# First pair's queries in a causal-attention and token-mixing kernel: one transfer and a turn on TensorE in place of four blocks and a turn on VectorE

## The chip, the cores and the metric

The kernel runs on one core of a Trainium2 chip. A core has five engines with their own in-order instruction streams (TensorE or PE for matrix products, VectorE or DVE, ScalarE or ACT, GpSimd or POOL, SyncE or SP, which here only issues transfers), and 16 DMA engines that carry the transfers of all queues. The metric is the time of one execution on the device in microseconds; lower is better.

## The reference

Inputs are q, k and v of shape (4, 12, 448, 64) and four weight matrices, all float32 (the token weights arrive as 8-byte floats and are narrowed in the kernel). Causal attention is followed by a mixer over tokens and one over channels:

```python
scores = q @ k.transpose(0, 1, 3, 2) / sqrt(64)          # 448 x 448 for each of 48 heads
scores = where(triu(ones, 1), -1e9, scores)
attn = exp(scores - max) / (sum + 1e-9)
x = (attn @ v).transpose(0, 2, 1, 3).reshape(4, 448, 768)
xt = x.transpose(0, 2, 1)
h = maximum(xt @ w_tok1, 0) @ w_tok2                      # over tokens: 448 -> 256 -> 448
u = x + h.transpose(0, 2, 1)
out = u + maximum(u @ w_ch1, 0) @ w_ch2                   # over channels: 768 -> 1536 -> 768
```

## The kernel before, in words

Heads are taken in 24 pairs: the 64 values of one head lie on partitions 0 to 63, of the other on 64 to 127. For each pair `load_pair` loads keys, queries and values; `prep` turns keys and queries so that the head dimension lies on partitions; `heads` makes the scores (line 1021, 32 small products in two jobs), masks them on VectorE (line 1043), takes exponentials on ScalarE (line 1055), sums and norms; `by_tensor` (pairs 0 to 9, line 1115) or `by_dma` turns the probabilities; `values` multiplies them with the values (lines 1245 and 1254). `xturn` and `tokens` mix tokens each time two head pairs of a batch are done (a third of its channels), and `channels` and `group` do the channel products (lines 1433, 1765, 1836, 1860), the bulk of the span. Everything is accumulated in PSUM and copied or added out of it by VectorE or ScalarE.

Keys and queries are turned in one of two ways. In the one of pair 0 and of pairs 6 and up, `load_pair.blocks` loads each tensor of a pair in four transfers (line 940) so that 32x32 blocks lie in place, and VectorE turns the blocks (`prep.turn`, line 988). In that of pairs 1 to 5 (`0 < g < WHOLE`), `load_rows` loads rows as they lie, in one transfer for pairs 1 and 2 (line 892, `g < ONCE`) and two for pairs 3 to 5 (line 895); TensorE turns them by products with the identity (`turn_rows.turn`, line 916 for pairs 1 and 2, 910 from pair 3), and VectorE or ScalarE copies the result out of PSUM (`turn_rows.evac`, through the helper `copy`, lines 632 and 634). Values are loaded by `load_pair.load` in three transfers (lines 949 and 953), and `load_pair.upper` copies a small part of them. `narrow` loads token weights (line 686).

The order of work is planned when the kernel is built. Each step is a job with costs, needs and buffers. `Plan.emit` walks a planned clock: each time an engine is free, it takes the ready job of lowest rank. The rank of a job is its place in a written list, `PLACES`, keyed by step, by the step's own number (twice the pair's number plus a constant) and by count; where several engines can do a job, a second list, `CHOICE`, gives the letter of the engine (a ScalarE, d VectorE, p GpSimd, s SyncE). Each engine runs its jobs in the order that the plan wrote. Constants of the plan are a transfer's lead (1320 ns), its time to land (1050 ns), and lags from engine to engine (145 ns from ScalarE).

Where the plan finds no ready job for TensorE in the first 75 us and little activity of late, it writes a filler (`keep_warm`, line 865): a product of 512 columns whose result is never read.

In pair 0, the keys go out on SyncE's queue and the queries on ScalarE's; the values of pair 0 follow on SyncE's queue, those of pair 1 on ScalarE's.

Of the kernel before, what the change touches and what calls it, by code (L numbers as in the profile page):

```python
# [21 lines left out]
    "load_pair.blocks": {-2: (0, 1), 10: (129, 153), 12: (193, 224), 14: (242, 259), 16: (338, 293), 18: (405, 420),  # L22
        20: (522, 537), 22: (578, 591), 24: (670, 694), 26: (742, 758), 28: (831, 851), 30: (911, 927), 32: (996,
        1006), 34: (1056, 1070), 36: (1141, 1151), 38: (1205, 1220), 40: (1280, 1293), 42: (1333, 1348), 44: (1406,
        1426)},
    "load_pair.load": {0.5: (2,), 2.5: (3,), 4.5: (178,), 6.5: (209,), 8.5: (274,), 10.5: (312,), 12.5: (393,),
        14.5: (453,), 16.5: (490,), 18.5: (558,), 20.5: (615,), 22.5: (704,), 24.5: (773,), 26.5: (822,), 28.5:
        (902,), 30.5: (949,), 32.5: (1047,), 34.5: (1114,), 36.5: (1194,), 38.5: (1241,), 40.5: (1376,), 42.5:
        (1441,), 44.5: (1489,), 46.5: (1531,)},
    "load_pair.upper": {-0.2: (12,), 1.8: (15,), 3.8: (213,), 5.8: (245,), 7.8: (317,), 9.8: (380,), 11.8: (441,),  # L30
        13.8: (505,), 15.8: (519,), 17.8: (592,), 19.8: (651,), 21.8: (727,), 23.8: (821,), 25.8: (859,), 27.8:
        (938,), 29.8: (982,), 31.8: (1077,), 33.8: (1136,), 35.8: (1226,), 37.8: (1269,), 39.8: (1401,), 41.8:
        (1462,), 43.8: (1517,), 45.8: (1561,)},
    "narrow.load": {3.5: (6, 9, 16, 62, 86, 121, 114, 144), 12: (288,), 13: (371,), 14: (445,), 15: (503,), 16:
        (606,), 17: (665,), 18: (755,), 19: (818,), 20: (897,), 21: (974,), 22: (1041,), 23: (1120,), 24: (1191,),
        25: (1254,), 26: (1328,), 27: (1400,), 28: (1463,), 29: (1511,), 30: (1553,), 31: (1599,), 32: (1627,), 33:
        (1660,), 34: (1687,), 35: (1730,)},
    "narrow.size": {3.5: (32, 52, 61, 116, 133, 177, 180, 235), 12: (352,), 13: (413,), 14: (484,), 15: (545,), 16:
        (642,), 17: (705,), 18: (786,), 19: (854,), 20: (932,), 21: (1013,), 22: (1072,), 23: (1153,), 24: (1223,),
        25: (1291,), 26: (1360,), 27: (1437,), 28: (1497,), 29: (1532,), 30: (1584,), 31: (1616,), 32: (1646,), 33:  # L40
        (1676,), 34: (1712,), 35: (1748,)},
    "narrow.shift": {3.5: (37, 56, 73, 125, 142, 183, 186, 263), 12: (359,), 13: (424,), 14: (491,), 15: (554,), 16:
        (646,), 17: (710,), 18: (793,), 19: (863,), 20: (939,), 21: (1019,), 22: (1084,), 23: (1157,), 24: (1227,),
        25: (1295,), 26: (1371,), 27: (1446,), 28: (1503,), 29: (1538,), 30: (1588,), 31: (1621,), 32: (1649,), 33:
        (1678,), 34: (1720,), 35: (1750,)},
    "narrow.join": {3.5: (40, 63, 80, 131, 146, 187, 194, 298), 12: (364,), 13: (436,), 14: (497,), 15: (587,), 16:
        (652,), 17: (724,), 18: (796,), 19: (870,), 20: (948,), 21: (1024,), 22: (1089,), 23: (1161,), 24: (1234,),
        25: (1300,), 26: (1374,), 27: (1450,), 28: (1505,), 29: (1543,), 30: (1590,), 31: (1623,), 32: (1655,), 33:
        (1681,), 34: (1725,), 35: (1755,)},
    "token_weights.<lambda>": {3.5: (44, 69, 85, 135, 150, 191, 201, 303)},  # L50
    "token_weights.rest_of": {3.5: (50, 74, 89, 139, 156, 195, 206, 310)},
    "prep.turn": {-1.5: (5, 8), 10.5: (199, 216), 12.5: (253, 271), 14.5: (286, 304), 16.5: (375, 384), 18.5: (449,
        486), 20.5: (562, 577), 22.5: (609, 626), 24.5: (702, 734), 26.5: (767, 790), 28.5: (877, 895), 30.5: (943,
        995), 32.5: (1014, 1034), 34.5: (1087, 1140), 36.5: (1166, 1176), 38.5: (1229, 1239), 40.5: (1304, 1315),
        42.5: (1368, 1378), 44.5: (1440, 1456)},
    "heads.<lambda>": {0: (11, 13), 2: (51, 57), 4: (94, 101), 6: (141, 160), 8: (197, 233), 10: (251, 267), 12:
# [3 lines left out]
    "heads.low": {0: (14, 20, 17, 21, 27, 25, 24), 2: (60, 78, 93, 75, 66, 70, 67), 4: (104, 109, 127, 112, 122,  # L60
# [9 lines left out]
    "heads.expo": {0: (18, 26, 22, 28, 41, 38, 34), 2: (65, 92, 102, 82, 72, 87, 77), 4: (110, 151, 155, 130, 140,  # L70
# [9 lines left out]
    "heads.guard": {0: (29, 47), 2: (107, 96), 4: (165, 145), 6: (215, 210), 8: (254, 280), 10: (307, 325), 12:  # L80
# [3 lines left out]
    "heads.recip": {0: (31, 53), 2: (111, 97), 4: (168, 154), 6: (226, 214), 8: (262, 284), 10: (315, 332), 12:  # L84
# [151 lines left out]
        2206, 2211)},  # L236
    "spared.hi": {-4.9: (2178, 2218)},
    "spared.lo": {-4.9: (2180, 2222)},
    "finish.plus": {-6: (2269, 2270, 2272, 2280)},
    "finish.turn": {-6: (2271, 2273, 2279, 2282)},  # L240
    "finish.evac": {-6: (2275, 2276, 2281, 2284)},
    "finish.send": {-6: (2277, 2278, 2283, 2285)},
# [1735 lines left out]
```

## Time and profile before

| | us |
|---|---|
| median of 3 runs | 537.71 |
| lowest and highest | 537.52 to 538.35 |
| the profiled execution's own time | 538.04 |
| its span, first to last instruction | 536.2 |
| TensorE busy | 529.8 |
| VectorE busy | 426.4 |
| ScalarE busy | 314.0 |
| GpSimd busy | 164.2 |

The profile is of one execution. A row of a timeline gives the start, the time, the engine, the line and what is written and read; queues of issuing engines have a q behind the engine (SPq). Matrix products are pipelined, so the busy time of one (373 ns for 448 columns) is longer than the distance to the next, and a busy TensorE is not TensorE at its peak. Fillers count as busy.

### The profile page before, as it was taken

What the parts mean: (1) busy time and instruction counts of PE and PEld (TensorE: products, weight loads), DVE (VectorE), ACT (ScalarE), POOL (GpSimd) and SP (SyncE); (2) the same over time, 40 slices, a digit from 0 to 9 for tenths busy, and PEclk for the clock granted to TensorE, in tenths of its full rate; (3) what the DMA queues carried; (4) which work ended last, traced back from release to release, by engine and by line L of the source; (5) the groups of instructions that cost most, each with busy time, mean ns of one, the idle gap of its engine ahead of it and who ended that gap; (6) DMA issues with size and microseconds to landing.
All of it is one profiled execution on the core that took longest, in us unless ns stands there. A gap on an engine that the chain in (4) does not pass through costs nothing.

```text
span 536.2 us, 12037 instructions
## 1 busy us (share of the span) xinstructions
PE 529.8 (99%) x4391; PEld 460.6 (86%) x4391; DVE 426.4 (80%) x1030; ACT 314.0 (59%) x768; POOL 164.2 (31%) x220
## 2 busy tenths in 40 slices
PE   8999999999999999999999999999999999999997
PEld 4778888888888888888898899999999999999996
DVE  5998899989797999888896679677877848485665
ACT  4998898899888787789784561243232313131300
POOL 2565745444252232332452132140010012321200
PEclk9999999999999999999999999999999999999999
DMA  9966677979999998999969327648213030212147
GB/s 194 198 116 144 152 214 160 215 153 233 207 178 200 225 190 193 205 196 229 210 163 198 115 92 205 131 119 162 88 32 116 7 91 23 87 32 88 31 75 131
DMA packets 221546, 77.72 MB, mean 145 GB/s; under 512 B 195760, under 2 KB 210992, under 8 KB 221488
## 3 DMA queue, kind: packets, MB, share of 16 engines
q1 hardware_dynamic: 207984, 74.90, 63.1%
q10 hardware_dynamic: 13504, 2.07, 2.1%
q8 instruction: 34, 0.56, 0.5%
q14 instruction: 24, 0.20, 0.2%
HBM read 49.15 MB, written 14.94 MB: 120 GB/s over the span
## 4 chain that ended last, share of the span: by engine, by line
PE 94%; SPq 2%; DVE 2%; ACT 1%; DMA 1%; issue 0%; POOL 0%; DVEq 0%; POOLq 0%
PE ps L1433 33%; PE ps L1860 16%; PE ps L1765 12%; PE ps L1021 6%; PE ps L1245 6%; PE ps L1383 6%; PE ps L1350 6%; PE ps L1836 3%; PE ps L1254 1%; PE ps L1115 1%; PE ps L1291 1%; SPq L940 1%; PE ps L865 1%; ACT prob L1055 1%; DMA gh<-in_k_dram 1%; PE ps L910 0%
## 5 line engine op out<-in xcount | busy, mean ns | idle before, releaser
L1500 DVE TENSOR_TENSOR u<-ps,u 128x448 f32<-128x448 f32 x118 | 72.5, 619 | 34.2 <-PE ps L1860 28.0
L1055 ACT ACTIVATE prob<-prob,stat 128x192 f32<-128x192 f32 (+6 forms) x168 | 83.7, 501 | 14.4 <-DVE stat L1043 14.1
L643 POOL TENSOR_TENSOR wl<-wf,wh 128x768 fp32r<-128x768 f32 x26 | 49.5, 1904 | 94.4 <-ACT wh L632 59.4
L1043 DVE CUSTOM_DVE_ANT_0 prob<-ps,mask 128x128 f32<-128x128 f32 (+6 forms) x168 | 63.3, 415 | 7.3 <-PE ps L1021 6.9
L634 POOL TENSOR_SCALAR prob<-prob,stat 128x64 f32<-128x64 f32 (+6 forms) x80 | 43.8, 559 | 55.4 <-DVE stat L1077 42.9
L1433 PE MATMUL ps<-uh,wh 128*128 128x448 f32 x144 | 53.7, 373 | 0.0
L1433 PE MATMUL ps<-gh,wh 128*128 128x448 f32 x144 | 52.9, 367 | 0.0
L1433 PE MATMUL ps<-gh,wl 128*128 128x448 f32 x144 | 52.7, 366 | 0.0
L1433 PE MATMUL ps<-gl,wh 128*128 128x448 f32 x144 | 52.7, 366 | 0.0
L1433 PE MATMUL ps<-uh,wl 128*128 128x448 f32 x144 | 52.7, 366 | 0.0
L1433 PE MATMUL ps<-ul,wh 128*128 128x448 f32 x144 | 52.7, 366 | 0.0
L632 ACT ACTIVATE wh<-wf 128x768 fp32r<-128x768 f32 x27 | 22.5, 846 | 51.2 <-PE ps L1860 25.8
L1021 PE MATMUL ps<-kq,kq 64*64 64x64 f32 (+5 forms) x768 | 45.4, 356 | 0.0
L1021 PEld LDWEIGHTS ps<-kq,kq 64*64 64x64 f32 x768 | 26.6, 133 | 15.5 <-issue 9.6
L1245 PE MATMUL ps<-pt,vraw 128*64 128x128 f32 (+2 forms) x544 | 37.3, 284 | 0.0
L1245 PEld LDWEIGHTS ps<-pt,vraw 128*64 128x64 f32 x544 | 28.2, 137 | 9.8 <-issue 2.1
L1795 DVE TENSOR_TENSOR kq<-kq,ps 128x448 f32<-128x448 f32 x35 | 21.2, 619 | 14.8 <-PE ps L1765 14.2
L1055 ACT ACTIVATION_READ_ACCUMULATOR prob<-prob,stat 128x1 f32 x168 | 32.1, 191 | 0.0
L638 ACT COPY pt<-pt 128x384 uint16<-128x384 uint16 (+3 forms) x41 | 31.6, 830 | 0.8 <-DMA pt<-prob 0.8
L1860 PE MATMUL ps<-u,wh 128*128 128x448 f32 (+1 forms) x110 | 31.0, 363 | 0.0
L1433 PEld LDWEIGHTS ps<-uh,wh 128*128 128x128 f32 x144 | 27.0, 188 | 2.8 <-issue 0.2
L1433 PEld LDWEIGHTS ps<-gl,wh 128*128 128x128 f32 x144 | 27.1, 188 | 2.5 <-DVE gl L1468 0.2
(222 smaller groups left out, 1403.2 us busy)
## 6 DMA issues: line engine op xcount, KB each, us to landing
wraw<-in_moe_w_ch_dram SPq DMA_DIRECT2D x24, 768.0 KB, 5.4
wf<-scratch SPq DMA_DIRECT2D x30, 384.0 KB, 3.1
scratch<-wf SPq DMA_DIRECT2D x24, 384.0 KB, 4.8
vraw<-in_v_dram SPq DMA_DIRECT2D x44, 96.0 KB, 3.4
kq<-in_k_dram SPq DMA_DIRECT2D x60, 56.0 KB, 3.7
kq<-in_q_dram SPq DMA_DIRECT2D x56, 56.0 KB, 2.4
out_dram<-h1l SPq DMA_DIRECT2D x24, 56.0 KB, 2.7
out_dram<-h1h SPq DMA_DIRECT2D x24, 56.0 KB, 2.2
```

Source lines behind the costliest of these rows:

```text
L634: eng[e].tensor_scalar(dst, src, scale, 0.0, op0=ALU.mult, op1=ALU.add)
L643: eng[e].tensor_tensor(dst, a, b, op=ALU.subtract)
L1021: nc.tensor.matmul(scores[n].tile[lanes, to:at], lhsT=qe.tile[LANES[j], c * QC:(c + 1) * QC], rhs=ke.tile[LANES[j], slice(*keys)], start=T ...
L1043: nc.vector.tensor_tensor_reduce(out=part(c, r), in0=ps.tile[:, at:at + wide(c)], in1=mask[:, S - QC:S + P] if c == 2 else mask[:, S - wid ...
L1055: nc.scalar.activation(part(c, r), part(c, r), AF.Exp, bias=stat.tile[:, 0, AT[c]:AT[c] + 1], scale=-1.0, accum_out=stat.tile[:, 1, AT[c]: ...
L1245: nc.tensor.matmul(to, lhsT=s.tile[:, kb, j], rhs=rhs, start=(n in first_of), stop=False)
L1350: nc.tensor.matmul(ps.tile[:, :PART], lhsT=w[:, c, m * P:(m + 1) * P], rhs=x.tile[:, c, :], start=(n == 0), stop=(n == len(work) - 1),)
L1383: nc.tensor.matmul(ps.tile[:, :S], lhsT=h.tile[:, m, o * P:(o + 1) * P], rhs=w[:, m, :], start=(n == 0), stop=(n == 3 * NM - 1),)
L1433: nc.tensor.matmul(ps.tile[:, :S], lhsT=x.tile[:, at_:at_ + P], rhs=y, start=(n == 0 and i == 0), stop=(n + 1 == w[2] and i == 2),)
L1500: eng[e].tensor_tensor(u, ps.tile[:, :S], u, op=ALU.add)
L1765: nc.tensor.matmul(ps.tile[:, :S], lhsT=l()[:, t * P:(t + 1) * P], rhs=r, start=(t == 0 and n == 0), stop=(t == half - 1 and n == 2),)
L1860: nc.tensor.matmul(ps.tile[:, cols], lhsT=l.tile[:, t * P:(t + 1) * P], rhs=r.tile[:, cols], start=(n == 0), stop=(n == 3 * len(fs) - 1),)
```

## The change

Pair 0's queries take the way of pairs 1 and 2: `load_rows` in one transfer, `turn_rows` on TensorE and a copy out of PSUM. Pair 0's keys stay with the blocks. The one transfer of pair 0's queries is issued on ScalarE's queue, where the four stood. Both lists are written anew over the whole kernel; the values of pair 0 are issued from ScalarE's queue in the new one. Cut to its core, with the head's places:

```diff
-    "load_pair.blocks": {-2: (0, 1), 10: (129, 153), ...
+    "load_pair.blocks": {-2: (1,), 10: (161, 98), ...
-    "load_rows.load": {0: (7, 4), 2: (10, 23), 4: (30, 45), 6: (68, 79), 8: (105, 91)},
+    "load_rows.load": {-2: (0,), 0: (3, 5), 2: (7, 22), 4: (13, 29), 6: (44, 74), 8: (82, 130)},
-    "load_pair.load": {0.5: (2,), 2.5: (3,), 4.5: (178,), 6.5: (209,), ...
+    "load_pair.load": {0.5: (2,), 2.5: (4,), 4.5: (146,), 6.5: (206,), ...
-    "narrow.load": {3.5: (6, 9, 16, 62, 86, 121, 114, 144), ...
+    "narrow.load": {3.5: (11, 20, 60, 64, 90, 141, 123, 180), ...
-    "prep.turn": {-1.5: (5, 8), 10.5: (199, 216), ...
+    "prep.turn": {-1.5: (8,), 10.5: (212, 252), ...
-    "turn_rows.turn": {0.5: (35, 19), 2.5: (64, 76), 4.5: (84, 90), 6.5: (117, 124), 8.5: (169, 148)},
+    "turn_rows.turn": {-1.5: (6,), 0.5: (17, 25), 2.5: (33, 68), 4.5: (62, 94), 6.5: (107, 151), 8.5: (135, 168)},
-    "heads.<lambda>": {0: (11, 13), 2: (51, 57), 4: (94, 101), 6: (141, 160), ... 20: (551, 557), ...
+    "heads.<lambda>": {0: (12, 14), 2: (47, 55), 4: (86, 100), 6: (139, 156), ... 20: (560, 574), ...
-    "values.pv": {0: (108, 132), 2: (173, 181), 4: (219, 223), ...
+    "values.pv": {0: (111, 119), 2: (174, 182), 4: (223, 229), ...
-    "tokens.tok1": {4.5: (257, 273), 8.5: (356, 367), 12.5: (506, 529), ...
+    "tokens.tok1": {4.5: (261, 284), 8.5: (361, 370), 12.5: (513, 539), ...
...
 CHOICE = {
-    "load_pair.load": {0.5: "s", 2.5: "a", 4.5: "s", ... 18.5: "a"},
+    "load_pair.load": {0.5: "a", 2.5: "a", 4.5: "s", ... 18.5: "s"},
-    "load_pair.upper": {-0.2: "d", 1.8: "p", 3.8: "p", ...
+    "load_pair.upper": {-0.2: "a", 1.8: "d", 3.8: "a", ...
-    "by_tensor.norm": {0: "dddapap", 2: "papapap", 4: "ppppapp", ...
+    "by_tensor.norm": {0: "dadpaap", 2: "ppdapap", 4: "pappapp", ...
-    "by_tensor.evac": {0: "dada", 2: "ddda", 4: "aaad", ...
+    "by_tensor.evac": {0: "dadd", 2: "ddda", 4: "aaad", ...
-    "turn_rows.evac": {0.5: "da", 2.5: "ad", 4.5: "ad", 6.5: "ad", 8.5: "ad"},
+    "turn_rows.evac": {-1.5: "d", 0.5: "dd", 2.5: "da", 4.5: "aa", 6.5: "ad", 8.5: "ad"},
-    "finish.evac": {-6: "ddad"},
+    "finish.evac": {-6: "dddd"},
...
@@ load_rows
         return s, [plan.job(
-            {"sp": 535.0 if g < ONCE else 1070.0}, load, holds=[home, s], rank=2.0 * g + RL,
+            {"sp" if g else "act": 535.0 if g < ONCE else 1070.0}, load, holds=[home, s], rank=2.0 * g + RL,
...
+    def lies(g, nm):
+        return nm != "v" and g < WHOLE and (g, nm) != (0, "k")
+
     def load_pair(g):
         b, t = divmod(g, NT)
         for nm, src in (("k", k), ("q", q), ("v", v)):
-            if 0 < g < WHOLE and nm != "v":
+            if lies(g, nm):
                 raws[g, nm] = load_rows(g, nm, src[b, 2 * t:2 * t + 2])
                 continue
...
@@ prep
         for nm, x in (("k", ke), ("q", qe)):
-            if 0 < g < WHOLE:
+            if lies(g, nm):
                 ready.append(turn_rows(g, nm, x))
                 continue
```

## Rows read from the trace of the kernel before

**Rows 1.** The page: span, busy time by engine, chain that ended last by engine.
```profile
span 536.2 us, 12037 instructions
PE 529.8 (99%) x4391; PEld 460.6 (86%) x4391; DVE 426.4 (80%) x1030; ACT 314.0 (59%) x768; POOL 164.2 (31%) x220
...
PE 94%; SPq 2%; DVE 2%; ACT 1%; DMA 1%; issue 0%; POOL 0%; DVEq 0%; POOLq 0%
```

**Rows 2.** Waits of TensorE's products, whole span: who waited for whom, us, times, longest.
```profile
PE ps L916 <- DMA uh<-in_k_dram: 0.7, 1, 0.7
```

**Rows 3.** Windows of the fillers (line 865) alone: stretch, us, busy (times) by engine.
```profile
0.00:8.40 8.40, 5.15 (x16) 1.84 (x16) 1.00 0.81 167
8.40:20.00 11.60, 1.81 (x6) 0.42 (x6) 1.00 1.07 217
20.00:45.00 25.00, 1.78 (x5) 0.40 (x5) 1.00 0.66 132
45.00:80.00 35.00, 0.00 (x0) 0.00 (x0) 1.00 0.71 179
```

**Rows 4.** Windows by stage: PE, PEld, DVE, ACT, POOL busy, granted clock, DMA share, GB/s.
```profile
8.40:20.00 11.60, 10.84 (x170) 7.40 (x170) 10.78 (x46) 11.60 (x40) 5.31 (x12) 1.00 1.07 217
20.00:45.00 25.00, 25.00 (x465) 19.58 (x457) 22.95 (x95) 24.22 (x84) 15.19 (x34) 1.00 0.66 132
```

**Rows 5.** Timeline of the head, 0 to 8.4 us: start, us, engine, line.
```profile
0.71 2.05 ACTq L940 DMA_DIRECT2D kq<-in_q_dram  x4
0.72 1.95 SPq L940 DMA_DIRECT2D kq<-in_k_dram  x4
...
2.82 1.05 SPq L949 DMA_DIRECT2D vraw<-in_v_dram  x2
...
4.37 0.73 SPq L953 DMA_DIRECT2D vraw<-in_v_dram  x1
4.46 1.69 PEld L865 LDWEIGHTS <-mask 128*128 128x128 bf16 x8 [0.28 <-issue]
...
4.94 1.17 DVE L988 STREAM_TRANSPOSE kq<-kq 128x448 f32<-128x448 f32 x2 [4.94 <-DMA kq<-in_k_dram]
...
6.57 1.79 PE L1021 MATMUL ps<-kq,kq 64*64 64x448 f32 x32
...
8.37 0.67 ACT L1055 ACTIVATE prob<-prob,stat 128x448 f32<-128x448 f32 x1 [1.77 <-DVE stat L1043]
```

**Rows 6.** Line 892: ns of an issue (min/median/max), and from issue to landing.
```profile
L892 SPq DMA_DIRECT2D ul<-in_q_dram x2: 437/478/519, 5.2 to 9.3; - x2
...
DMA to landing us min/median/max: 3.1/5.0/5.6
```

**Rows 7.** Timeline: TensorE's turn of pair 1's queries, and a copy from PSUM.
```profile
8.44 0.99 PE L916 MATMUL ps<-ident,ul 112*64 112x112 f32 x16
...
12.10 0.62 DVE L634 TENSOR_SCALAR kq<-ps 128x448 f32<-128x448 f32 x1
```

**Rows 8.** DMA queues from 2 to 5 us: packets, MB, share of 16 engines.
```profile
DMA packets 4184, 0.60 MB, mean 201 GB/s; under 512 B 4184, under 2 KB 4184, under 8 KB 4184
...
q10 hardware_dynamic: 2116, 0.30, 59.4%
q1 hardware_dynamic: 2068, 0.30, 58.8%
```

**Rows 9.** Timeline from 6.3 to 13 us: pair 1's load, turn and products.
```profile
6.37 0.43 SPq L892 DMA_DIRECT2D uh<-in_k_dram  x1
...
9.36 0.82 PE L865 MATMUL ps<-mask 128*128 128x512 bf16 x3
...
10.87 0.99 PE L916 MATMUL ps<-ident,uh 112*64 112x112 f32 x16 [0.68 <-DMA uh<-in_k_dram]
...
12.90 0.59 PE L1021 MATMUL ps<-kq,kq 64*64 64x448 f32 x4
```

**Rows 10.** Timeline of the tail: the last copy out of PSUM.
```profile
532.91 0.42 DVE L634 TENSOR_SCALAR kq<-ps 112x256 f32<-112x256 f32 x1 [0.52 <-PE ps L1893]
```

More of the change, by code (lines that the diff above doesn't have):

```diff
@@ L21 @@
 PLACES = {
[L22 to L56, printed above, removed]
[3 rows of a table removed]
@@ L237 @@
[L237 to L242, printed above, removed]
+    "load_pair.blocks": {-2: (1,), 10: (161, 98), 12: (185, 237), 14: (219, 254), 16: (325, 288), 18: (409, 423),
+        20: (516, 533), 22: (580, 598), 24: (664, 686), 26: (742, 756), 28: (818, 837), 30: (902, 920), 32: (995,
+        1008), 34: (1059, 1078), 36: (1125, 1138), 38: (1191, 1208), 40: (1254, 1273), 42: (1325, 1344), 44: (1411,
+        1424)},
@@ new lines @@
+    "token_weights.<lambda>": {3.5: (66, 85, 112, 138, 160, 209, 225, 263)},
+    "token_weights.rest_of": {3.5: (71, 89, 117, 143, 165, 213, 228, 266)},
+    "prep.turn": {-1.5: (8,), 10.5: (212, 252), 12.5: (272, 277), 14.5: (286, 297), 16.5: (371, 375), 18.5: (452,
+        467), 20.5: (564, 571), 22.5: (627, 637), 24.5: (704, 723), 26.5: (765, 786), 28.5: (860, 871), 30.5: (939,
+        994), 32.5: (1024, 1030), 34.5: (1091, 1100), 36.5: (1160, 1177), 38.5: (1222, 1233), 40.5: (1283, 1302),
+        42.5: (1352, 1370), 44.5: (1446, 1456)},
@@ new lines @@
+    "values.evac": {0: (136,), 2: (198,), 4: (258,), 6: (310,), 8: (403,), 10: (466,), 12: (492,), 14: (561,), 16:
+        (616,), 18: (655,), 20: (716,), 22: (793,), 24: (876,), 26: (944,), 28: (1031,), 30: (1089,), 32: (1162,),
+        34: (1236,), 36: (1306,), 38: (1390,), 40: (1458,), 42: (1531,), 44: (1619,), 46: (1653,)},
+    "xturn.turn": {1: (218,), 5: (324,), 9: (474,), 13: (588,), 17: (667,), 21: (811,), 25: (960,), 29: (1094,), 33:
+        (1240,), 37: (1400,), 41: (1535,), 45: (1659,)},
@@ new lines @@
+    "xturn.none": {1: (256,), 5: (353,), 9: (501,), 13: (644,), 17: (708,), 21: (841,), 25: (997,), 29: (1127,), 33:
+        (1277,), 37: (1418,), 41: (1576,), 45: (1673,)},
+    "tokens.tok1": {4.5: (261, 284), 8.5: (361, 370), 12.5: (513, 539), 16.5: (651, 660), 20.5: (761, 767), 24.5:
+        (850, 882), 28.5: (1034, 1063), 32.5: (1168, 1186), 36.5: (1312, 1319), 40.5: (1421, 1429), 44.5: (1596,
+        1602), 48.5: (1680, 1687)},
+    "tokens.relu": {-5: (280, 299, 373, 381, 526, 552, 666, 674, 771, 779, 877, 892, 1049, 1083, 1179, 1196, 1324,
+        1336, 1435, 1455, 1604, 1610, 1684, 1694)},
@@ new lines @@
+    "by_dma.split": {20: (608, 628, 623, 631), 22: (688, 705, 717, 724), 24: (776, 772, 800, 799), 26: (848, 851,
[3 rows of a table added]
+    "by_dma.turn": {20: (632, 654), 22: (709, 729), 24: (780, 804), 26: (856, 885), 28: (936, 952), 30: (1018,
+        1032), 32: (1090, 1099), 34: (1163, 1170), 36: (1226, 1243), 38: (1301, 1309), 40: (1372, 1379), 42: (1453,
+        1463), 44: (1521, 1532), 46: (1586, 1611)},
+    "merged.merge": {20: (670, 673, 695, 694), 22: (739, 744, 760, 766), 24: (805, 813, 843, 834), 26: (909, 910,
[3 rows of a table added]
@@ new lines @@
+    "add.plus": {-6: (743, 751, 734, 763, 801, 809, 1055, 1113, 1080, 1069, 1137, 1149, 1190, 1130, 1228, 1259,
[6 rows of a table added]
+    "store.turn": {-5: (1755, 1781, 1779, 1797, 1790, 1811, 1841, 1839, 1864, 1856, 1879, 1873, 2233, 2237, 2241,
+        2245, 2249, 2253, 2254, 2258, 2263, 2267)},
+    "store.send": {-5: (1757, 1787, 1782, 1800, 1794, 1813, 1850, 1842, 1867, 1859, 1883, 1875, 2234, 2238, 2243,
+        2246, 2252, 2255, 2261, 2259, 2266, 2268)},
+    "reread.load": {-4.95: (1834, 1847), -4.94: (1857, 1865, 1899, 1901), -4.93: (1914, 1942, 1976, 1979), -4.92:
+        (1994, 1999, 2038, 2039), -4.91: (2060, 2063, 2101, 2103), -4.9: (2127, 2130, 2168, 2169, 2179, 2206)},
@@ new lines @@
+    "combined.sum_.do": {-4.94: (1882, 1885, 1888, 1890), -4.93: (1956, 1959, 1963, 1968), -4.92: (2018, 2021, 2024,
+        2028), -4.91: (2086, 2087, 2090, 2092), -4.9: (2146, 2151, 2158, 2161)},
+    "group.product.do": {55.44: (1880,), 55.71: (1898,), 55.98: (1903,), 56.25: (1913,), 56.52: (1925,), 56.79:
[5 rows of a table added]
+    "group.first.do": {-6: (1887, 1949, 2059, 2089, 2150)},
+    "group.plus.do": {-6: (1906, 1917, 1919, 1931, 1935, 1943, 1941, 1993, 1995, 1998, 2002, 2004, 2008, 2014, 2062,
+        2064, 2067, 2070, 2073, 2074, 2077, 2129, 2131, 2138, 2140, 2142, 2144, 2148, 2189, 2190, 2205, 2207, 2209,
+        2215, 2210)},
@@ L243 @@
+    "spared.hi": {-4.9: (2174, 2216)},
+    "spared.lo": {-4.9: (2176, 2220)},
+    "finish.plus": {-6: (2270, 2271, 2273, 2281)},
+    "finish.turn": {-6: (2272, 2274, 2280, 2283)},
+    "finish.evac": {-6: (2276, 2277, 2282, 2285)},
+    "finish.send": {-6: (2278, 2279, 2284, 2286)},
 }
@@ L279 @@
[L279 to L281 removed]
[3 rows of a table removed]
[L285 to L288 removed]
+    "xturn.none": {1: "p", 5: "a", 9: "a", 13: "a", 17: "a", 21: "a", 25: "a", 29: "p", 33: "p", 37: "a", 41: "p",
+        45: "a"},
@@ L289 @@
+    "merged.merge": {20: "ddda", 22: "aaaa", 24: "aada", 26: "daad", 28: "dada", 30: "ddaa", 32: "adda", 34: "dada",
+        36: "daad", 38: "ddaa", 40: "addd", 42: "daaa", 44: "aaad", 46: "adda"},
+    "mixtures.mix.lo": {48.6: "pdpddppddddp"},
[3 rows of a table added]
+        -4.92: "adap", -4.91: "adap", -4.9: "adap"},
+    "combined.split.lo": {-4.94: "dpdd", -4.93: "pddd", -4.92: "ddpp", -4.91: "dpdd", -4.9: "ppdd"},
+    "spared.lo": {-4.9: "dd"},
+    "finish.evac": {-6: "dddd"},
 }
```

213 lines of the change are left out of this document (98 added, 115 removed), and 203 rows, old and new, of tables (CHOICE, PLACES).

## The prediction, written before the change was timed

> **What bounds the kernel now.** I read the page first. TensorE is busy for 529.8 of the 536.2 us and carries 94% of the chain that ended last [rows 1]; the longest wait of a matmul on another engine or a DMA, after the start, is the 0.7 us on a load of keys [rows 2]. The kernel is TensorE's stream from one end to the other, and an edit elsewhere moves the time only if it makes that stream start earlier, run emptier fillers, or stall. But a busy share hides fillers, the matmuls of line 865 that keep TensorE active and compute nothing. So I read the windows of that line next: 16 of the 27 stand ahead of the first product, six between 8.4 and 20 us, five until 45 us, none later [rows 3]. Time can therefore come from the head, and hardly from elsewhere.
>
> The windows by stage say who TensorE waits for there. Between 8.4 and 20 us ScalarE is busy 11.60 of 11.60 us, VectorE 10.78; until 45 us 24.22 and 22.95 of 25.00 [rows 4]. After 8.4 us the pace is set by those two, and a load that comes earlier is worth only what they can take up.
>
> Then the head itself [rows 5]. Keys (SyncE's queue) and queries (ScalarE's) each go out as four transfers between 0.71 and 2.76 us. VectorE begins with the keys at 4.94, takes both turns in 1.17 us and is done at 6.11. The first product starts at 6.57, 0.46 us later, because fillers already queued on TensorE run until then: TensorE is in order. The first exponential is at 8.37, and from there ScalarE is full.
>
> **The change part by part.** All sums are made against the profiled execution, 538.04 us (span 536.2 and 1.8 around it); the median of the runs is 537.71, 0.33 below, and I carry the differences over to it.
>
> *The turn.* VectorE loses a block transpose (two took 1.17 us) and gains a copy of 448 columns out of PSUM, 0.62 us in the nearest row [rows 5, 7]: nothing, within 0.05. TensorE gains the 16 small matmuls of line 916, 0.99 us [rows 7]. They lie where fillers run, so they cost nothing while the queries are there first; without that cover they cost up to their 0.99.
>
> The Trainium skill speaks against this edit: "VectorE: DVE Perf Modes", section "The three transpose paths" and the rules after it, has VectorE as the fastest for turns of 32x32 blocks and notes that TensorE's lands in PSUM. The rows agree on the price, 0.62 against 0.99 and 0.62; by the rule alone, with queries and keys landing together, the first product would be 0.99 later.
>
> *The queries' load.* One issue instead of four. The same form on SyncE's queue (line 892) takes 0.44 to 0.52 us to issue, and 3.1 to 5.6 us from issue to landing [rows 6], the long ends where much was queued ahead. With nothing ahead, issued at 0.71, I take the low end: landed by 3.8 to 4.2, before the keys. TensorE then turns them as soon as its fillers let it. The list's own due time, made of its constants (0.70 start, 1.32 lead, 1.04 transfer, 1.05 landing, 0.15 lag), is 4.26, so only the fillers before it stand ahead, eight of the sixteen, whose pace is the slow one until 4.46 [rows 5]: turn from about 4.7 to 5.7.
>
> *The keys* stay as they are, four issues on SyncE until 2.67, but their companion changes: the pair's values, three issues on SyncE's queue before (2.82 to 5.10), now follow the queries on ScalarE's queue, from about 1.2. Between 2 and 5 us the two queues split the DMA engines 58.8 to 59.4 [rows 8], and ScalarE's queue was as full with the queries' blocks as it now is with queries and values. So the keys keep their half, and I take 4.94 to 5.3 for VectorE's start on them, 5.15 in the sum. To that the keys' turn, 0.62, the copy of the queries behind it on VectorE, 0.62, and 0.1 of hand-over: first product at 6.5, bounds 6.25 and 6.7, against 6.57. Gain 0.1 us (0.3 to -0.1). The 0.46 us that fillers cost before is gone, and VectorE's two turns in a row are late next.
>
> The Trainium skill, "DMA: Bandwidth & Descriptors", section "Queues, rings and completion order", says that each DMA engine goes round the queues that have work, packet by packet. The split of 58.8 to 59.4 agrees; the values moved to ScalarE's queue then cost the keys no share, and by this rule alone the keys would start at 4.94 again.
>
> *Three issues moved off SyncE.* The next loads of SyncE come sooner: pair 1's keys, issued at 6.37 before, behind the values, its queries and a weight, now directly behind the first keys, at about 2.7. Before, TensorE stood 0.7 us for them with 0.82 us of fillers ahead, and took them at 10.87 [rows 2, 9]. Both can go: 1.5 us of TensorE. But the next product of that pair came at 12.90, after VectorE's copy at 12.10 and ScalarE's [rows 9], with ScalarE full all the time [rows 4]. The time freed on TensorE becomes wait unless ScalarE's and VectorE's work shrinks, which the edit leaves equal. Bounds: gain 1.5, gain 0; I take 0.1, near the saturated rows. ScalarE's queue has seven issues in the head either way (four and three before; one, three, three after): nothing. Pair 0's small value copy moves from VectorE to ScalarE, which is idle before 8.37: nothing. What is queued behind SyncE's earlier loads are the token weights, later by one or two loads of about 1.1 us; their first product stands at list place 257 and has tens of microseconds: nothing.
>
> *The refitted list.* Some 2,280 jobs keep their work and change place by about ten on average, and several hundred choices of engine change. Its own words do not show a lead: pair 1's first product moves from place 51 to 47, pair 2's from 94 to 86, but pair 0's values from 108 to 111, the first token product from 257 to 261, and pair 10's scores from 551 to 560. In the first two pairs VectorE gets two operations of about 0.6 us more (block turns and turn copies 3 to 4, evacuations 5 to 6, norms 3 and 3, value copies 1 and 1), and ScalarE, the fuller of the two, one turn copy and one evacuation less and one value copy more. After 45 us there is no filler left and only stalls can change. Bounds: gain 2.4, the eleven later fillers at some 0.22 each [rows 3, 9], loss 1.2, two such operations of VectorE on a saturated stretch. Nothing here is nearer to one end; I take a gain of 0.2, since places 47 and 86 are about a half microsecond early at some five jobs a microsecond, and most of it is given back.
>
> *The tail.* One of the last copies of 256 columns goes from ScalarE to VectorE, whose own such copy takes 0.42 us and which stands idle for 0.52 before it [rows 10]. It fits: nothing.
>
> Sum: 0.1 + 0.1 + 0.2 = 0.4 us less, **537.3 us**.
>
> **The rivals.**
> *The head's loads pay (faster).* If pair 1's products really move up with their loads, the 1.5 us of fillers and wait after 9.36 go, with the 0.3 of the first product: 537.71 - 1.8 = 535.9. For it: the only long wait of TensorE is there. Against it: ScalarE full from 8.37. With the refit a mixture between this and the forecast passes the 1.1 us. Chance 0.35.
>
> *The first keys are pushed back by the values (slower).* The values' 224 KB, at the 201 GB/s of that stretch [rows 8], are 1.1 us. If they all go ahead of the keys' last block, VectorE starts on the keys at 6.05, the first product at 7.4, 0.85 later than before; ScalarE's full stretch shifts with it, and with one of VectorE's two extra operations felt, 0.6, the end is 1.4 later: 539.1. It decides once VectorE starts on the keys later than about 5.2, and costs what exceeds that. Late queries do the same: at the 5.6 us end of their landing they arrive at 6.3, turn and copy end at 8.0. If they land only with the keys, TensorE's turn is bare and costs its 0.99 (this is the skill's rule above): 538.7. For it: the engines are full from 2 us on. Against it: the even split. Chance 0.20.
>
> *It does not do what it says*: the queries are in early, but the first product still waits for the keys, turned no sooner. That is inside the forecast: 537.4 to 537.7.
>
> **How the numbers follow.** A measurement of this kernel (537.52 to 538.35) tells about 0.2%, 1.1 us, from no change. Forecast with its own bounds (536.7 to 538.7) 0.45, faster rival 0.35, slower 0.20. The range reaches from 535.6, a little below the faster rival, to 538.9, most of the slower one: 8 in 10. Faster 0.35, same 0.45, slower 0.20.
>
> **What would show it.** Right: one issue of queries on ScalarE's queue, line 916 on TensorE at 4.7 to 5.0, the block transpose of line 988 once in the head from 4.9 to 5.3, the first product of line 1021 at 6.25 to 6.7, ScalarE full from about 8.3, no 0.7 us wait on pair 1's keys, line 865 again some 20 to 27 times, and 45 us on with the same work as before. Wrong: the keys' turn after 5.5, line 916 waiting on a DMA for over half a microsecond, ScalarE with idle time before 20 us, fillers after 8.4 us down to a few (the faster rival) or well over eleven (the slower), or new stalls of TensorE after 80 us, which only the refit can bring.

## The result, and the profile after

The changed kernel takes 542.59 us (median of 9 runs, 540.21 to 545.15) against 537.73 for the kernel before on the same chip: a ratio of 1.0091, 95% interval 1.0075 to 1.0107. It is slower by about 4.9 us, outside the forecast range (535.6 to 538.9). Its profiled execution took 541.43 us, with a span of 539.5; the one of before took 538.04, with 536.2 [rows 1]. The profiles therefore hold 3.3 of the 4.9 us.

The page of the changed kernel (span; busy time of each engine; chain that ended last):

```profile
span 539.5 us, 12025 instructions
...
PE 532.3 (99%) x4403; PEld 460.9 (85%) x4403; DVE 428.9 (79%) x1046; ACT 320.4 (59%) x775; POOL 156.1 (29%) x197
...
PE 90%; DMA 4%; DVE 3%; ACT 2%; SPq 1%; issue 0%; POOL 0%; DVEq 0%; ACTq 0%; POOLq 0%
```

Against [rows 1], GpSimd has 23 operations fewer (220 to 197), VectorE 16 more and ScalarE 7 more: the new list moved 23 operations, net, from the idlest engine to the two fuller ones. TensorE's count is 12 larger: 16 products of the turn more, 4 fillers fewer (27 before, 23 now).

The head of the changed kernel in its timeline, to be laid beside [rows 5]:

```profile
0.71 0.43 ACTq L892 DMA_DIRECT2D ul<-in_q_dram  x1
0.72 2.70 SPq L943 DMA_DIRECT2D kq<-in_k_dram  x4
1.17 1.15 ACTq L952 DMA_DIRECT2D vraw<-in_v_dram  x2
...
4.16 1.76 PE L916 MATMUL ps<-ident,ul 112*64 112x112 f32 x16
...
4.71 0.31 SPq L892 DMA_DIRECT2D uh<-in_k_dram  x1
...
6.18 0.65 DVE L991 STREAM_TRANSPOSE kq<-kq 128x448 f32<-128x448 f32 x1 [6.18 <-DMA kq<-in_k_dram]
...
6.75 0.58 DVE L634 TENSOR_SCALAR kq<-ps 128x448 f32<-128x448 f32 x1
...
7.52 1.79 PE L1024 MATMUL ps<-kq,kq 64*64 64x448 f32 x32
...
9.31 0.67 ACT L1058 ACTIVATE prob<-prob,stat 128x448 f32<-128x448 f32 x1 [1.98 <-DVE stat L1046]
```

The queries are in early: TensorE turns them from 4.16 us. But the four issues of the keys now stretch over 2.70 us (1.95 before), VectorE begins on the keys at 6.18 (4.94 before), and the first product starts at 7.52 (6.57 before). The head is 0.95 us late, as in the slower rival of the prediction. That looks like the answer, and it isn't: the next views put the loss elsewhere.

A TensorE that looks busy all the time hides a loss; the busy time of its weight loads (PEld) does not, since each product has one and their total is nearly the same in both kernels (460.6 and 460.9 us). In a stretch it says how much of the stream got done. Windows by stage (stretch, length, then busy time and count of PE, PEld, DVE, ACT, POOL; clock, DMA share, GB/s), first the kernel before, then the changed one:

```profile
60.00:160.00 100.00, 100.00 (x1151) 85.10 (x1150) 91.96 (x259) 90.43 (x246) 46.40 (x63) 1.00 0.90 186
160.00:200.00 40.00, 40.00 (x366) 33.97 (x365) 34.61 (x102) 32.65 (x79) 11.60 (x16) 1.00 1.05 201
```

```profile
60.00:160.00 100.00, 99.31 (x1126) 82.27 (x1125) 91.54 (x256) 90.63 (x242) 39.23 (x52) 1.00 0.85 182
160.00:200.00 40.00, 40.00 (x364) 33.95 (x363) 36.16 (x109) 32.82 (x85) 12.83 (x16) 1.00 1.07 203
```

Between 60 and 160 us the changed kernel gets 2.83 us less of TensorE's stream done (82.27 against 85.10), while VectorE and ScalarE are as busy as before and GpSimd 7 us less. From 160 us on the two are equal. The same can be followed step by step: to the time reached in an execution I added the usual distance of every product still to start (fillers at nothing), and compared the sum with that of before. The changed kernel is behind by 0.8 us at 8 us, 0.0 at 55, 0.9 at 80, 1.4 at 120, 3.1 at 160 and 2.8 at the end. Up to 80 us these figures move by up to 0.8 us with how the small products are weighted, so they don't tell how much of the head's lag is left at 55 us; from 120 us on they hold to 0.1. Most of the loss comes after 60 us. The last 0.3 us of the 3.3 are in the tail: from the start of the last copy to the end of the span pass 3.62 us, against 3.29 before [rows 1, 10]. Not all of that need come from the list: f3, a run described below that keeps the order of before, has 3.49 there. The copy in the timeline of the changed kernel:

```profile
535.88 0.42 DVE L634 TENSOR_SCALAR kq<-ps 112x256 f32<-112x256 f32 x1 [0.19 <-DMA out_dram<-kq]
```

### The profile page after: what moved, and what is told of

Same layout as the page of the kernel before. It is cut to its first block, busy times and chain, and to the rows that moved or that the text cites. A ratio compares the mean times of both kernels' runs of the same rounds, so it can differ in the third digit from the quotient of the medians.

```text
span 539.5 us, 12025 instructions
## 1 busy us (share of the span) xinstructions
PE 532.3 (99%) x4403; PEld 460.9 (85%) x4403; DVE 428.9 (79%) x1046; ACT 320.4 (59%) x775; POOL 156.1 (29%) x197
## 4 chain that ended last, share of the span: by engine, by line
PE 90%; DMA 4%; DVE 3%; ACT 2%; SPq 1%; issue 0%; POOL 0%; DVEq 0%; ACTq 0%; POOLq 0%
PE ps L1436 30%; PE ps L1863 16%; PE ps L1768 12%; PE ps L1024 7%; PE ps L1248 6%; PE ps L1353 5%; PE ps L1386 5%; PE ps L1839 3%; PE ps L1118 2%; PE ps L865 1%; PE ps L1257 1%; PE ps L1294 1%; DMA pt<-prob 1%; DMA kq<-in_k_dram 1%; ACT pt L638 1%; DVE prob L1046 1%
## 5 line engine op out<-in xcount | busy, mean ns | idle before, releaser
L1058 ACT ACTIVATE prob<-prob,stat 128x64 f32<-128x64 f32 (+6 forms) x168 | 83.9, 503 | 10.7 <-DVE stat L1046 10.4
L643 POOL TENSOR_TENSOR wl<-wf,wh 128x768 fp32r<-128x768 f32 x23 | 44.4, 1929 | 114.1 <-ACT wh L632 112.8
L1046 DVE CUSTOM_DVE_ANT_0 prob<-ps,mask 128x256 f32<-128x256 f32 (+6 forms) x168 | 63.2, 415 | 7.3 <-PE ps L1024 7.1
L634 POOL TENSOR_SCALAR prob<-prob,stat 128x192 f32<-128x192 f32 (+6 forms) x70 | 37.9, 550 | 54.9 <-DVE stat L1080 45.4
L638 ACT COPY pt<-pt 128x384 uint16<-128x384 uint16 (+3 forms) x46 | 36.5, 861 | 4.4 <-DMA pt<-prob 4.4
L1248 PEld LDWEIGHTS ps<-pt,vraw 128*64 128x64 f32 x544 | 28.2, 137 | 10.3 <-issue 2.8
L632 ACT ACTIVATE prob<-prob,stat 128x384 f32<-128x384 f32 (+6 forms) x60 | 28.0, 493 | 3.5 <-DVE stat L1080 3.4
```

Source lines behind the costliest of these rows:

```text
L632: nc.scalar.activation(dst, src, AF.Copy, scale=scale)
L634: eng[e].tensor_scalar(dst, src, scale, 0.0, op0=ALU.mult, op1=ALU.add)
L638: nc.scalar.copy(out, in_)
L643: eng[e].tensor_tensor(dst, a, b, op=ALU.subtract)
L1046: nc.vector.tensor_tensor_reduce(out=part(c, r), in0=ps.tile[:, at:at + wide(c)], in1=mask[:, S - QC:S + P] if c == 2 else mask[:, S - wid ...
L1058: nc.scalar.activation(part(c, r), part(c, r), AF.Exp, bias=stat.tile[:, 0, AT[c]:AT[c] + 1], scale=-1.0, accum_out=stat.tile[:, 1, AT[c]: ...
```

## The experiments

Two things could make the kernel slow: the head (keys late, values on ScalarE's queue) or the rewritten list. Each run was timed beside the kernel before; a ratio is to that, with its 95% interval.

**First, one part of the change at a time, with the kernel's own plan.** e1 gives the values of pair 0 back to SyncE's queue by their letter in the list:

```diff
-    "load_pair.load": {0.5: "a", 2.5: "a", ...
+    "load_pair.load": {0.5: "s", 2.5: "a", ...
```

> The changed kernel with one letter put back: pair 0's values go out on SyncE's queue behind the first keys, as before, and not on ScalarE's behind the queries. Theory A (the 256-byte packets of queries and values on ScalarE's queue hold back the keys' blocks on SyncE's, 76% to 45% of the engines between 2 and 5 us): VectorE starts the keys at 5.0 to 5.3 and not at 6.18, the first product is at 6.4 to 6.7 and not at 7.52, and the time falls by about 1 us from the changed kernel's 542.6, to about 541.6; if all of the loss hangs on the late head, to 538. Theory B (the loss is the refitted list's order further on): first product earlier, time still 542 to 543.

Measured: 548.72 us, ratio 1.0203 (1.0189 to 1.0217). The keys' turn started at 6.03, the first product at 7.89.

e2 has the new head in the list of before, with places for the three new steps (load 0, turn 4.5, copy 8) and the values of pair 0 on SyncE's queue:

```diff
-    "prep.turn": {-1.5: (5, 8), ...
+    "prep.turn": {-1.5: (5,), ...
+    "turn_rows.turn": {-1.5: (4.5,), 0.5: (35, 19), ...
```

> The queries' edit alone: the list of the kernel before, with the queries' load, turn and copy at the places of the four blocks and their turn (0, 4.5, 8), values of pair 0 on SyncE's queue. Theory A: the queries' single transfer has only its own 896 packets on ScalarE's queue, so the keys are started by 5.0 to 5.4 and the first product is at 6.4 to 6.8; time 537.3 to 538.3. Theory B: 537.5 to 538, the edit is neutral. A third (the turn on TensorE itself costs): line 916 waits or runs slow and the first product is after 7; time 538.7 or more.

Measured: 546.18 us, 1.0154 (1.0133 to 1.0174); first product at 7.16.

e3 has the new list and the old head (queries in four blocks, turned by VectorE); e4 is e3 with the values of pair 0 on SyncE's queue:

```diff
-            if lies(g, nm):
+            if 0 < g < WHOLE:
```

> The refitted list alone: queries of pair 0 as four blocks on ScalarE's queue again and turned on VectorE at the copy's place (9), everything else in the new list's order, values of pair 0 on ScalarE's queue behind the queries. Theory A: the keys have to share with 128-byte packets of the queries first, so they start at 4.9 to 5.2 and the first product at 6.5 to 6.7; time 1 us below the changed kernel, 541.5, or 538 if the head is all. Theory B: time stays at 541 to 543, since the list is the loss.

> As the list alone, with the values of pair 0 on SyncE's queue: the head of the kernel before, the order of the new list behind it. Theory A with the head as the whole loss: 537.5 to 538.5. Theory B: 541 to 543, the same as with the values on ScalarE's queue.

Measured: e3 544.09 us, 1.0119 (1.01 to 1.0139), e4 547.80 us, 1.019 (1.0173 to 1.0207). e3 is no clean test of the head: its plan put the values ahead of the queries on ScalarE's queue, the queries' turn waited till 8.06 us and the first product came at 8.76.

All four are slow, whichever part they keep, and all lie above the 542.59 of the whole change, e3 by no more than the spread of the runs. Only e2 came out inside a range of its expectation, the open one of its third theory, that the turn on TensorE costs; f3 below, with the same turn, does not bear that out. What they share is that any edit of a job, even one letter, sends the plan on another walk: compared row by row in the traces, of some 6860 products, other operations and issues about 400 in e1 and in e4 stand elsewhere than in the changed kernel (about 50 in e3), and about 660 in e2 elsewhere than in the kernel before. So none of the four undid one thing alone. From here the order was held fixed.

**The head and the order, crossed.** f3 keeps the order of before, job for job, and only its head differs: where the plan issues the four blocks, one transfer goes into a spare buffer; after the sixth filler TensorE turns it; where VectorE turned the blocks it copies the result; the values go to ScalarE's queue; the fillers 12 to 16 are left out, for the room that the turn takes.

```diff
     def keep_warm(e):
+        calls[0] += 1
+        if 12 <= calls[0] <= 16:
+            return
         nc.tensor.matmul(rest, lhsT=still[:, :P], rhs=still, start=True, stop=True)
+        if calls[0] == 6:
+            ... the 16 products of the turn
             def load(e, s=s, src=src):
+                e = "act" if g < 2 else e
```

> The order of the kernel before on every engine, job for job, with the head of the changed one: queries of pair 0 in one transfer, turned on TensorE after six fillers, five fillers more before the first product, values of pair 0 behind the queries on ScalarE's queue. Theory H (the late keys are the loss and spread): keys start near 6.1, first product near 7.5, time 541 to 543. Theory O (the order that the refit and the planner made is the loss): the head is late by the same 1 us but the time is only that much above before, 538.5 to 539.2.

Measured: 538.05 us, ratio 0.9998 (0.9985 to 1.0012), although the keys' turn started at 6.30, the first product at 7.65 and the first exponential at 9.44, all later than in the changed kernel. That is less than either theory had expected: theory O had the late head cost about 1 us.

f4 is the mirror: the changed kernel's order, job for job, with the queries as four blocks in a spare buffer, turned by VectorE where it copied, and nothing turned on TensorE.

```diff
+            if g == 0:
+                nc.vector.transpose(make(x, [P, S], F32), qblocks.rearrange("p c d -> p (c d)"))
+                return
             copy(e, make(x, [P, S], F32), ps.tile[:, :S])
```

> The order of the changed kernel on every engine, job for job, with the queries of pair 0 as four blocks on ScalarE's queue and turned on VectorE where the copy stood; TensorE's turn is left out; values of pair 0 stay behind the queries on ScalarE's queue. Theory H: keys start at 4.9 to 5.2, first product near 6.6, time 537.5 to 538.5. Theory O: the head is as before, but the time only falls by the 1 us of the head, to 541 to 542.

Measured: 542.66 us, 1.0081 (1.0055 to 1.0106), with the first product at 6.38. By itself f4 does not clear the head for every engine: in the new order ScalarE copies a part of pair 0's values before its first exponential, in f4 it waits for them until 7.39, and so its first exponential comes at 9.12, nearly as late as in the changed kernel (9.31). It is f3 that shows such a start of ScalarE, at 9.44, to cost nothing measurable.

| | order of before | new order |
|---|---|---|
| four blocks, VectorE | 537.98 (before) | 542.66 (f4) |
| one transfer, TensorE | 538.05 (f3) | 542.59 (changed kernel) |

The changed kernel's 542.59 comes from its first timing; timed once more beside f3 and f4 it took 541.86 (a2, below). The loss goes with the column. The windows of f3 and then of f4, in the stretch that lost, say the same:

```profile
60.00:160.00 100.00, 99.90 (x1150) 84.74 (x1149) 91.89 (x257) 89.65 (x244) 47.04 (x65) 1.00 0.88 187
```

```profile
60.00:160.00 100.00, 98.91 (x1126) 82.27 (x1126) 89.42 (x258) 90.72 (x241) 38.59 (x50) 1.00 0.84 182
```

f4, with the old head, does 82.27 us of weight loads there, as the changed kernel does.

**What holds the keys back.** f1 keeps the new order and head, but issues the values physically on SyncE's queue behind the keys; a2 is the changed kernel once more, beside it.

```diff
             def load(e, s=s, src=src):
+                e = "sp" if g < 2 else e
```

> The order of the changed kernel with nothing but the issue of the values of pairs 0 and 1 moved to SyncE's queue, behind the keys that stand ahead of them there; ScalarE's queue carries the queries' one transfer alone. If the values' packets hold back the keys, these start at 5.0 to 5.3 again; if the queries' 896 packets of 256 bytes do it by themselves, at 5.6 or later. First product accordingly at 6.5 or at 7.0 and later. Time: theory H 538 to 539.5 if the keys are on time; theory O 541.5 to 542.5.

> The changed kernel once more, for a second profile and its spread beside the three others: 540 to 545, median 542 to 543; keys start near 6.2, the first product at 7.2 to 7.6. Theory H says that slower executions of it have a later first product; theory O that the first product is at the same place and the difference lies further on.

Measured: f1 542.24 us, 1.0077 (1.0052 to 1.0102); a2 541.86, 1.0067 (1.0042 to 1.0093). With the queries alone on ScalarE's queue the keys' turn still started at 5.66. That alone would be thin evidence, since with the queries as four blocks ahead of any values it started anywhere from 4.94 to 5.58 (before, e4, f4, h2 and g1). The packets between 2.5 and 3.0 us show why (queue: packets, MB; q1 is SyncE's, q10 ScalarE's), in the kernel before, in the changed one and in f1:

```profile
q10 hardware_dynamic: 387, 0.05, 62.1%
q1 hardware_dynamic: 372, 0.05, 59.2%
```

```profile
q10 hardware_dynamic: 536, 0.14, 120.0%
q1 hardware_dynamic: 37, 0.00, 5.7%
```

```profile
q10 hardware_dynamic: 514, 0.13, 115.2%
q1 hardware_dynamic: 45, 0.01, 7.1%
```

In this half microsecond of the queries' one transfer the keys nearly stop, with the values beside it or not. The values add a second part: the keys' fourth issue waits until 3.10 us in the changed kernel, and goes out at 2.19 in f1 and in the kernel before. What it waits for is in the trace. The program counts landings with eight counters (semaphores) that both queues share, and an issue that gets a used counter waits until the transfer that had it has landed. In the changed kernel eight issues go out ahead of the keys' fourth, which gets the counter of the keys' first transfer; pair 1's first two loads (line 892) then wait for values of pair 0. The waits of SyncE's queue up to 8 us (who waited for what: us, times, longest):

```profile
SPq L892 <- DMA vraw<-in_v_dram: 1.8, 2, 1.3
SPq L943 <- DMA kq<-in_k_dram: 0.9, 1, 0.9
```

f1's first product came at 8.82, 2.44 later than in f4, but not for its keys, which were turned by 6.31: the queries' turn started at 5.04, and the fillers behind it ran until then. The two take the same time within their spread (541.04 to 544.71 and 541.03 to 544.43, six runs each). In the profiled executions f1's span is 1.0 us longer (540.4 against 539.4). So in the new order, too, a part of a late head is free; how much of the 2.44 us, these runs don't resolve.

**What the head is worth in the old order.** g1 is the kernel before with the values alone moved to ScalarE's queue (the last line of f3's diff); e5 is the same move made by the letter in the list, so that the plan walks anew; g2 is f3 with nine fillers more ahead of the first product.

```diff
-    "load_pair.load": {0.5: "s", 2.5: "a", ...
+    "load_pair.load": {0.5: "a", 2.5: "a", ...
```

> The kernel before, order job for job, queries still as four blocks turned on VectorE; only the three transfers of pair 0's values are issued on ScalarE's queue behind the queries. Theory O (the order of the work from 60 us on sets the time; the head has room): 537.3 to 538.3. Theory H (a change in the head's loads by itself costs or gains): 536.5 or less if the earlier loads of SyncE count, 539 or more if the first keys are held back.

> The same change of queue as in the run beside it, but made by the letter in the list of the kernel before (0.5: s to a), so that the planner walks its clock again and writes another order behind it (some 580 of 5010 rows of the engines' streams differ). Theory O: with an order that nobody fitted the time rises to 541 to 547, although the head is the same as in the run beside it. Theory H: the two are equal within 0.5 us.

```diff
+        if calls[0] == 11:
+            for _ in range(9):
+                nc.tensor.matmul(rest, lhsT=still[:, :P], rhs=still, start=True, stop=True)
```

> The order before with the changed head, as in the run that cost nothing, and nine fillers more ahead of the first product, which moves it from 7.65 to 9 to 9.6 us, 2.5 to 3 us later than in the kernel before. If the head's room is what the loads of pairs 6 and up leave (TensorE waits for them near 45 us), the room is about 1.5 us and the time is 538.5 to 539.8; if there were no room after the first 1.1 us, 539.5 to 540; with room for all of it, 538.

Measured: g1 538.93 us, 1.0016 (0.9998 to 1.0034); e5 547.01, 1.0174 (1.0151 to 1.0198); g2 539.63, 1.0027 (1.0015 to 1.0039). The same queue for the same three transfers costs at most 1.8 us in the old order and 9 us where the plan may react to it; e5's plan changed the head as e3's did (queries' turn at 8.13), but by the reckoning above e5 is 3.4 to 5.2 us behind at 45 us, and 8.5 at the end. g2's first product came at 9.58, 3.0 later than before and 1.93 later than in f3, and it costs 1.6 us against f3: most of it. So in the old order a little over a microsecond of the head is free, and no more. g1's 538.93 lies between the ranges of its two theories, and its interval just reaches 1.

Where f3 makes up its microsecond can be read in products that all three kernels have, because the order is the same. The timeline of before, of f3 and of g2:

```profile
36.83 0.99 PE L1021 MATMUL ps<-kq,kq 64*64 64x448 f32 x12
...
42.70 0.65 DVE L988 STREAM_TRANSPOSE kq<-gh 128x448 f32<-128x448 f32 x1 [1.18 <-DMA gh<-in_k_dram]
...
45.83 0.65 PE L1115 MATMUL ps<-ident,prob 64*128 64x64 f32 x13 [0.41 <-DVE stat L1043]
...
46.91 1.05 PE L1021 MATMUL ps<-kq,kq 64*64 64x320 f32 x20
```

```profile
37.69 0.99 PE L1044 MATMUL ps<-kq,kq 64*64 64x448 f32 x12
...
42.28 0.62 DVE L1011 STREAM_TRANSPOSE kq<-gh 128x448 f32<-128x448 f32 x1
...
46.89 1.05 PE L1044 MATMUL ps<-kq,kq 64*64 64x320 f32 x20
```

```profile
39.60 0.99 PE L1047 MATMUL ps<-kq,kq 64*64 64x448 f32 x12
...
48.81 1.05 PE L1047 MATMUL ps<-kq,kq 64*64 64x320 f32 x20
```

At 37 us f3 is 0.86 behind before, ten microseconds later it is level, and g2 went from 2.77 to 1.90 behind. The kernel before loses that time here, most of it ahead of the product at 45.83 us: VectorE stands 1.18 us for the keys of a later pair, its mask pass comes late and TensorE waits for it. f3 and g2 have no such wait. A head that is early by a microsecond runs into a load that isn't. g1, with an early head (first product at 6.80), has no wait here but one of 0.52 us ahead of a product at 58.13, behind another load of keys that VectorE waited 1.75 us for (timeline of g1):

```profile
56.11 0.65 DVE L989 STREAM_TRANSPOSE kq<-gh 128x448 f32<-128x448 f32 x1 [1.75 <-DMA gh<-in_k_dram]
```

Whether f3 escapes both because its stream comes later or because SyncE issues earlier (the load of keys that VectorE waits for at 42.70 in the kernel before went out at 37.65 there, at 36.13 in f3 and at 37.25 in g1) is not settled.

**Which half of the list.** A list has places and engines. h1 keeps the new places, with the plan walked as in the changed kernel, and runs each of the 278 jobs whose engine letter differs on the engine of before; h2 is the mirror, the order of before with those jobs on the new engines.

```diff
-                pick.fn(e)
+                pick.fn(getattr(pick, "run_on", e))
```

> The changed kernel, its order of jobs planned as it is, but each of the 278 jobs of copies, norms and adds whose engine the new list chose otherwise runs on the engine of the list of before (85 go back to GpSimd, 62 leave it). Theory 'the engines' (23 operations net were moved from GpSimd to VectorE and ScalarE, and TensorE waits for these two): about 538.5, 537.5 to 539.5, weight loads of 84.5 us or more between 60 and 160 us. Theory 'the places' (the order of the jobs of TensorE, VectorE and ScalarE costs, whoever runs them): about 542.3, 541 to 544, weight loads of 82.3 us there. Theory 'both were fitted to one another': above 543, up to 548, weight loads of 82 us or fewer.

> The mirror of it: the kernel before, order and head as they are, the same 278 jobs on the engines of the new list. Theory 'the engines': about 542, 541 to 544, weight loads of 82.5 us between 60 and 160 us against 85.1 before. Theory 'the places': about 538, 537.2 to 539, weight loads of 84.8 us or more. Theory 'both were fitted to one another': 541 to 546, as for the other of the two, so that both cross pairs are slower than both matched pairs or near the slower.

| | engines of before | new engines |
|---|---|---|
| places of before | 538.17 (before) | 547.70 (h2) |
| new places | 550.84 (h1) | 542.59 (changed kernel) |

Ratios 1.0236 (1.0214 to 1.0258) for h1 and 1.0169 (1.0146 to 1.0193) for h2. Neither half is the cause by itself. With the engines of before the new places cost 12.7 us, with the places of before the new engines cost 9.5, and the two together 4.9 (542.59 against the 537.73 beside it): the halves fit only one another. The two crossed kernels are orders that nobody fitted, as those of e1 to e5 are, so they don't tell what either half would cost with a partner made for it. The theory of the engines falls most plainly in h1, which gives GpSimd its operations back and does 80.05 us of weight loads in the stretch that lost, less than the changed kernel; its window, then that of h2:

```profile
60.00:160.00 100.00, 97.23 (x1088) 80.05 (x1084) 89.05 (x239) 85.42 (x232) 44.55 (x62) 1.00 0.81 180
```

```profile
60.00:160.00 100.00, 96.57 (x1145) 80.18 (x1143) 90.56 (x254) 88.84 (x234) 39.90 (x51) 1.00 0.86 185
```

No run beat the kernel before.

## Why the prediction was wrong, point by point

*What bounds the kernel.* TensorE's stream does. But "Time can therefore come from the head, and hardly from elsewhere" was the wrong turn. The fillers of line 865 show where TensorE had nothing to do, not where the end is set: f3's head is 1.08 us late and costs nothing measurable, and of g2's 3.01 us only 1.6 are felt. Windows of the fillers of the changed kernel, against [rows 3]:

```profile
0.00:8.40 8.40, 4.47 (x11) 1.26 (x11) 1.00 0.85 171
8.40:20.00 11.60, 1.04 (x4) 0.31 (x4) 1.00 1.10 234
20.00:45.00 25.00, 2.59 (x8) 0.69 (x8) 1.00 0.66 137
```

They are 23, as forecast (20 to 27), and they say nothing about the 4.9 us.

*The turn and the queries' load* came out about as forecast. One issue at 0.71; turned from 4.16 to 5.92 (six fillers stood ahead of it, not eight), before the keys were there, so that the turn costs nothing; 1.76 us instead of the 0.99 of [rows 7], because it ran at the lower clock.

*"So the keys keep their half"* is the step of the head that failed. The split of 58.8 to 59.4 [rows 8] was read off two queues with transfers of equal size, 448 packets of 128 bytes on either side (56 KB each). One transfer of 896 packets of 256 bytes doesn't share like that: from 2 to 5 us the changed kernel has 1978 packets of ScalarE's queue and 1643 of SyncE's, 76.2 to 44.7% of the engines' time, and in the half microsecond above 536 to 37. The Trainium skill, "DMA: Bandwidth & Descriptors", section "Queues, rings and completion order", says that an engine drains a whole packet of many descriptors from one queue before it goes to the next. (The packets that the rows count are single pieces of 128 or 256 bytes, not packets in the page's sense.) The prediction had used the first half of that rule, the turns, and dropped the second, their length. Turns of one length on both queues would not give 536 to 37; no row here shows how long a turn is, so whether their length is the cause stays open. The second delay of the keys, the wait of their fourth issue for a counter, the prediction did not have.

*The slower rival* had the mechanism of the head right (keys at 6.05, first product at 7.4; measured 6.18 and 7.52) and half of its cause: the queries' own transfer holds the keys back too, and what the values add is at least in part the late fourth issue. In e3 and e5, where the values stood ahead of four blocks of queries, that issue went out at 3.37 and 3.42 and the keys' turn started at 6.00 and 6.14. Its price was wrong. "ScalarE's full stretch shifts with it" is true, the first exponential moved from 8.37 to 9.31, but the end doesn't shift, since what follows waits for something else: in before for loads of keys at 42 and 55 us. In f4, with the early head, TensorE gives its lead of 1.14 us over the changed kernel back at once. Its waits after the first product, up to 60 us (who waited for whom: us, times, longest), then that of the changed kernel:

```profile
PE ps L1134 <- DVE prob L634: 1.3, 1, 1.3
...
PE ps L929 <- DMA uh<-in_k_dram: 0.9, 1, 0.9
```

```profile
PE ps L1118 <- DVE prob L634: 0.9, 1, 0.9
```

That is 2.2 us against 0.9.

*Three issues moved off SyncE.* Pair 1's keys went out at 4.71 instead of 6.37, not at 2.7 as forecast, because their issue waited for the landing of pair 0's first values, whose counter it has; the 0.7 us wait for them went. "The time freed on TensorE becomes wait" held: no gain is seen.

*The refitted list* is the term that failed: taken at a gain of 0.2, with a loss of at most 1.2, it measured 4.7 us (f4 against before, 542.66 to 537.98). The bound was made of operations counted in the first two pairs, as if a list could lose only by the work it adds to a full engine. The count of the whole span, 23 operations off GpSimd, wasn't made; and it wouldn't have done either, since h1 gives them back and is slower. What the traces show in place of it is TensorE waiting more often. Weight loads of TensorE that waited 0.2 us or more between 60 and 160 us add up to 7.2 us in before and 7.4 in f3, but 10.5 in the changed kernel, 9.9 in a2, 10.5 in f4 and 10.3 in f1; waits on VectorE make 0.9 to 1.5 of it with the new order, 0.0 and 0.2 with the old, and 1.1 to 2.1 more are waits with no releaser shown. These are mostly short waits, of 0.2 to 0.5 us, spread over many lines. "After 45 us there is no filler left and only stalls can change" said where to look, and the sum then gave that stretch no price of its own. One of the prediction's own signs of being wrong, new stalls of TensorE after 80 us "which only the refit can bring", is what came: from 80 to 160 us the changed kernel's lag grows from 0.9 at most to 3.1.

*The tail* was set at nothing. It took 0.3 us longer in the changed kernel's profile (3.62 against 3.29), but 0.2 longer in f3's (3.49), whose tail is that of before, so no cost of the new list is shown there.

Open stays which places of the new order between 60 and 160 us cost what: h1 and h2 say that places and engines can't be priced apart. Open, too, is why executions of the changed kernel spread from 540.2 to 545.2. One candidate is seen and not shown: near 121 us TensorE waits for a copy that ScalarE makes of probabilities turned by DMA, 0.3 us in the changed kernel and 1.0 in f4's execution:

```profile
PEld ps L1264 <- ACT pt L638: 1.0, 1, 1.0
```

## What to carry to other kernels

Where a plan writes the order of a whole kernel, judge an edit by transplanting it into the old order, job for job, before believing any time: here the edit itself cost nothing measurable, and seven other orders, replanned or half refitted, took 6 to 13 us more than the order of before. A refitted order is a change of its own, to be given bounds of several microseconds either way. And before pricing a late or early head, look for the next place where the stream waits for something that doesn't start in the head; up to there a shift of about a microsecond was free here.

## What the runs showed of the hardware beyond that

The fillers start at 1.49 us in these kernels, at a distance of 0.43 us, which is 512 columns at 1.2 GHz, and later run at 0.22 us, 2.4 GHz. (The granted clock of the windows reads 1.00 in the whole head, so the distance is what tells.) The pace changed at 4.61 us in the kernel before, at 4.24 in f4, 6.86 in the changed kernel, 5.82 in a2, which is the same kernel again, 7.12 in f3 and 8.6 in f1. The turn is not needed for a late change: h2 has the head of before, with the same fillers back to back from 1.49 us on, and its pace changed at 7.30, so that its first product came at 7.90 and not at 6.57. What the pace does shows in the five fillers behind the turn, in the changed kernel, in a2 and in f1:

```profile
5.86 1.73 PE L865 MATMUL ps<-mask 128*128 128x512 bf16 x5
```

```profile
5.90 1.25 PE L865 MATMUL ps<-mask 128*128 128x512 bf16 x5
```

```profile
6.74 2.15 PE L865 MATMUL ps<-mask 128*128 128x512 bf16 x5
```

Two executions of one kernel differ by half a microsecond on the same five products, so a time in the head is worth little to the tenth from one profile. The price of TensorE's turn hangs on it, too: its 16 products took 0.99 us at 2.4 GHz [rows 7], 1.76 at 1.2 GHz, and 1.30 in e2.
